# The first head pair's choice of clusters in two halves of 384 queries and 384 keys

## The chip, the cores and the metric

The kernel runs on one core of a Trainium2 chip. The time is the device time of one execution in microseconds (us). The time before is the median of three runs, 702.19 us (699.18, 702.19 and 703.92).

Engines: TensorE (PE in the profile, its weight loads PEld), VectorE (DVE), ScalarE (ACT), GpSimd (POOL) and SyncE (SP, which here only issues transfers).

## What is computed

Attention in which a query sees only the keys of its own cluster, and behind it a mixture of experts in which each row goes to one expert:

```python
# q, k, v: (4, 8, 768, 64); centroids: (8, 16, 64); x: (3072, 512); 8 experts of 512 x 1024 x 512
q_assign = np.argmax(np.einsum('bhsd,hcd->bhsc', q_n, c_n), axis=-1)
k_assign = np.argmax(np.einsum('bhsd,hcd->bhsc', k_n, c_n), axis=-1)
mask = q_assign[:, :, :, None] == k_assign[:, :, None, :]
scores = scale * np.matmul(q, k.transpose(0, 1, 3, 2))
scores = np.where(mask, scores, -1000000000.0)
...
return np.matmul(attn, v).astype(np.float32)
...
logits = xn @ en.T / tau
expert_idx = np.argmax(logits, axis=1)
...
h = np.maximum(x[mask] @ w1[e], 0.0)
out[mask] = gate_w[mask, None] * (h @ w2[e])
```

Here q_n, k_n, c_n, xn and en are rows divided by their length, attn is the softmax of the scores and gate_w the softmax of the logits at the chosen expert.

## The kernel before

The 32 pairs of batch and head are worked through as 16 pairs of heads (n = 0 to 15), two heads side by side in the 128 rows of TensorE. Of each pair, 768 queries are taken in two halves of 384 (`hq`), and for each half the 768 keys in six blocks of 128 (`j`). One such block is a *unit*; there are 12 to a pair, and the main loop takes two units a step (`it` = 0 to 5). For a unit, `scores` fills one tile of PSUM (s_ps, L519) from two parts: part 1 is the product of k and q (f32), part 0 the product of the *table* H (bf16, `hot` in the profile), which adds a large negative number where the clusters of query and key differ. `expo` (L530, ScalarE) makes the exponential, `attend` (L541) multiplies by v on TensorE, and VectorE sums the exponentials for the softmax (L550 and L560).

The table of a pair is made in *pieces*, which stand in the program ahead of the pair's own units:

- *turn*: q and k are turned so that the head's 64 numbers lie along the partitions. From pair 1 on VectorE does it in blocks of 32 (L402). For pair 0 TensorE turns them with the identity (L383) and VectorE and ScalarE copy the results out of PSUM (L389, L393).
- *products* (L412): the product with the unit centroids, cnB, four matmuls of 384 columns (two halves of q, two of k), then a transpose by VectorE into asn (L421).
- *choose* (L430 to L433, VectorE): the largest of 16 per row, as a number pm.
- *codes* (L438, L442): from pm the entries of cd, for queries and keys; the constant entries of cd are written once, in `constants`.
- the table: cd turned. From pair 1 on a transposing transfer does it (L456); for pair 0 TensorE does (L467, `turn_numbers`), and VectorE and ScalarE copy parts of it into `hot` (L474 to L479).

In pair 0, before, the two halves of k's turned columns are not natural halves: `in_halves` places alternate groups of 32 keys, and v is loaded in the matching order (eight transfers, L196).

The start is written out by hand in `begin()`, and the whole attention stage runs under a manual schedule: every engine runs its instructions in the order of the program text. TensorE first runs ten dummy products (`keep_up`, L233), later six more while the choice is made. A transfer is issued by an engine's own queue (here SP's or ScalarE's); its end is told by one of eight semaphores that are used in turn, so that an issue can wait for the end of the transfer that had its semaphore before. `misc()` gives two PSUM banks in turn; psS has two more for the scores (used for q's turn at the start), and unit 2's scores at the start take a tile of the values products' pool.

The changed places by line: `load` L190, `keep_up` L229, `constants` L252, `unit_centroids` L301, `unit_experts` L313, `turned_experts` L318, `begin` L328, `turn` L373, `choose` L423, `codes` L436, `turn_numbers` L458, `scores` L499, `between` L1369 and the main loop from L1430.

Of the kernel before, what the change touches and what calls it, by code (L numbers as in the profile page):

```python
# [39 lines left out]
def kernel(  # L40
# [144 lines left out]
    def load(n, names):  # L185
        b, hp = pairs[n]
        t = ld.setdefault(n, {})
        for nm in names:
            x = t[nm] = ldp.tile([P, NJ, 2, D], F32, tag=nm + "32", name=nm + "32")
            for h in range(2):  # L190
                rows = {"q": q, "k": k, "v": v}[nm][b, 2 * hp + h]
                if nm == "v":
# [7 lines left out]
                if n == 0:  # L200

                    for i in range(1 + (nm == "k")):
                        js = slice(NJ // 2 * i, NJ // 2 * i + NJ // 2) if nm == "k" else slice(0, NJ)
                        queue = nc.scalar if nm == "k" and i == 0 else nc.sync
                        queue.dma_start(
                            out=x[:, js, h], in_=rows.rearrange("(j p) d -> p j d", p=P)[:, js]
                        )
                    continue


# [42 lines left out]
    def constants():  # L253
        nc.vector.memset(onesb, 1.0)
        keep_up(10, idle_ps[:, 0])
# [45 lines left out]
    def unit_centroids():  # L301
        unit_rows(cn_r)
        nc.vector.tensor_scalar(cn2, bc(c_sb, [P, 2, D], 1), cn_r, None, ALU.mult)
        bk = misc()
# [8 lines left out]
    def unit_experts():  # L313
        unit_rows(en_r)
        nc.vector.reciprocal(tau, tau)
        nc.vector.tensor_scalar(emb, emb, en_r, tau, ALU.mult, ALU.mult)

    def turned_experts():  # L318
# [5 lines left out]
        nc.vector.tensor_copy(  # L324
# [3 lines left out]
    def begin():  # L328

        nc.scalar.dma_start(out=c_sb, in_=centroids.rearrange("h c d -> (h c) d"))  # L330
        load(0, "q")
        load(0, "k")
        nc.sync.dma_start(out=emb, in_=moe_expert_emb)
        nc.sync.dma_start(out=tau, in_=moe_tau.to_broadcast([E, 1]))
        load(0, "v")
        load(1, "qk")
        constants()

        nc.scalar.activation(en_r, epsc[0:E], ACTF.Sqrt)
        norm_rows(cn_r, c_sb, P)  # L340
        unit_centroids()
        piece(0, "turn0")
        piece(0, "turn1")
        norm_rows(en_r, emb, E)

        nc.scalar.activation(cn_r, epsc, ACTF.Exp)
        piece(0, "products")
        for m in range(2):
            scores(m, (1,))
        un[2]["s_ps"] = psO.tile([P, 2, 512], F32, tag="o_ps", name="s_ps2")  # L350
        scores(2, (1,))
        piece(0, "choose")
        piece(0, "codes")
        keep_up(6, misc())
        unit_experts()
        rest = piece(0, "turn_numbers")
        next(rest)
        for m in range(3):
            scores(m, (0,))
        next(rest, None)  # L360
        turned_experts()
        for m in (0, 2, 1):
            expo(m)
        token_numbers()

    def prep_pieces(n):
# [8 lines left out]
        def turn(nm, half):  # L375
# [12 lines left out]
            if nm == "q":  # L388
                (nc.vector.tensor_copy if half else nc.scalar.copy)(  # L389
                    t["qT"][:, HS * half : HS * half + HS], bk[:, 0:HS]  # L390
                )
            else:
                (nc.scalar.copy if half else nc.vector.tensor_copy)(  # L393
                    in_halves(t["kT"])[:, half], bk[:, 0:HS].rearrange("p (s t) -> p s t", t=SQ)
                )
# [27 lines left out]
        def choose():  # L423
# [3 lines left out]
            amax = smp.tile(shp[0:2], F32, tag="amax", name="amax")  # L427
            sel = smp.tile(shp, BF16, tag="sel", name="sel", bufs=1)
            pm = smp.tile(shp[0:2], BF16, tag="pm", name="pm")
# [6 lines left out]
        def codes():  # L436
            pm = t["pm"]
            nc.scalar.activation(cd[..., 1], pm, ACTF.Copy, scale=wcd)  # L438
# [1249 lines left out]
```

## Time and profile before

| | us |
|---|---|
| median of three runs | 702.19 |
| the profiled execution | 699.54 |
| its span | 697.7 |
| TensorE busy in the span | 684.7 (98%) |
| VectorE, ScalarE, GpSimd busy | 381.4, 261.5, 252.7 |
| granted TensorE clock, mean of the span | 0.999 |

The profile is of one execution. A page gives the busy time of each engine, the chain of work that ended last, followed back from the end, and groups of instructions by line; a row of a group has the count, the busy time in us, the mean of one in ns, and the idle time ahead of it with what ended it. The trace behind it can be asked for any stretch. In the first 16 us, by the timeline (start, length):

| | us |
|---|---|
| dummies of L233 | 1.07, 3.71 |
| centroids turned, L305 | 5.17, 0.30 |
| q turned, L383 | 5.33, 0.85 |
| k turned, L383, two halves | 6.12 and 6.89, 0.52 each |
| centroid products, L412 | 7.38 to 8.82 |
| asn, L421 | 8.85, 0.58 |
| amax, is_equal, product, pm, L430 to L433 | 9.47, 10.05, 10.64, 11.04 |
| codes on VectorE, L442, two | 11.70, 0.53 |
| cd turned, L467 | 12.38, 0.83 |
| copies to the table, L474 to L479 | 13.15 to 14.19 |
| scores, part 0, units 0 to 2 | 13.95, 0.68 |
| exponentials of units 0, 2, 1, 3 | 14.36, 2.92 |
| attend of units 0 and 1 | 16.03, 1.80 |

### The profile page before, as it was taken

To read this page: it belongs to the slowest core of one execution; us is meant where nothing else is said; L and a number is where in the kernel's file an instruction comes from. 1 tells how busy PE (TensorE), PEld (TensorE's weight loads), DVE (VectorE), ACT (ScalarE), POOL (GpSimd) and SP (SyncE) were. 2 spreads that over 40 slices of the span, in tenths; PEclk is the share of its full clock that TensorE was granted. 3 is DMA by queue.
4 is the path that set the end of the run, shared out by engine and by line. 5 is a ranking of instruction groups with operands and counts; after the bars stand their busy time and mean duration, and the time that the engine had idled before them with its cause. 6 is when DMAs were issued, how large, how long until landed. Compare 5 with 4: busy or idle time off the path is not lost.

```text
span 697.7 us, 16185 instructions
## 1 busy us (share of the span) xinstructions
PE 684.7 (98%) x6517; PEld 459.1 (66%) x6517; DVE 381.4 (55%) x667; ACT 261.5 (37%) x443; POOL 252.7 (36%) x439
## 2 busy tenths in 40 slices
PE   8999999999999999999999999998999999999996
PEld 4444444444444444456776678887979797979694
DVE  6788998998899999988563121240210303030310
ACT  5656655577666765576142120101010111111111
POOL 2122222321132222361216256736364554635402
PEclk9999999999999999999999999999999999999999
DMA  8755566875578587699699957457777686879450
GB/s 136 121 90 108 103 98 82 163 142 104 107 134 165 122 154 149 173 277 260 171 357 353 348 172 284 158 192 244 260 249 268 218 296 236 294 265 317 143 226 32
DMA packets 244156, 135.55 MB, mean 194 GB/s; under 512 B 207840, under 2 KB 207842, under 8 KB 244076
## 3 DMA queue, kind: packets, MB, share of 16 engines
q1 hardware_dynamic: 237116, 121.10, 63.9%
q0 software_dynamic: 6016, 13.12, 5.2%
q8 instruction: 54, 0.88, 0.6%
q10 hardware_dynamic: 944, 0.23, 0.2%
q14 instruction: 26, 0.21, 0.1%
HBM read 115.92 MB, written 13.12 MB: 185 GB/s over the span
## 4 chain that ended last, share of the span: by engine, by line
PE 89%; issue 4%; DMA 3%; POOL 1%; DVE 1%; another core or an unknown queue 1%; POOLq 0%; ACT 0%; DVEq 0%
PE s_ps L519 22%; PE o_ps L541 18%; PE h_ps L1303 10%; PE y_ps L1319 10%; PE h_ps L1217 9%; PE y_ps L1254 5%; PE misc L1254 5%; PE x_ps L1217 3%; DMA out_dram<-ys,spidx 3%; PE misc L591 2%; PE misc L412 2%; PE misc L670 1%; POOL out_dram L1090 0%; POOL xin L1079 0%
## 5 line engine op out<-in xcount | busy, mean ns | idle before, releaser
L530 ACT ACTIVATE prob<-s_ps 128x768 f32<-128x768 f32 x192 | 154.1, 814 | 100.8 <-PE s_ps L519 99.9
L519 PE MATMUL s_ps<-qT,kT 64*64 64x384 f32 x1536 | 155.6, 482 | 0.0
L541 PE MATMUL o_ps<-prob,v 64*64 64x385 f32 x1536 | 141.2, 483 | 0.0
L560 DVE TENSOR_TENSOR acc<-acc,prob 128x768 f32<-128x768 f32 x128 | 121.6, 950 | 8.5
L541 PEld LDWEIGHTS o_ps<-prob,v 64*64 64x64 f32 x1536 | 58.4, 133 | 65.0 <-issue 57.8
L1263 DVE STREAM_TRANSPOSE ys<-y_ps 128x256 f32<-128x256 f32 (+4 forms) x16 | 6.5, 414 | 156.8 <-PE y_ps L1254 141.1
L1303 PE MATMUL h_ps<-xTm,w1s 128*128 128x128 f32 x768 | 89.0, 276 | 1.2 <-issue 1.2
L1303 PEld LDWEIGHTS h_ps<-xTm,w1s 128*128 128x128 f32 x768 | 87.6, 192 | 3.0 <-issue 2.6
L1319 PE MATMUL y_ps<-w2s,hT 128*128 128x512 f32 x192 | 84.5, 593 | 0.0
L1090 POOL DMA_INDIRECT out_dram<-ys,spidx x56 | 56.3, 1005 | 74.7 <-DVE ys L1277 58.7
L519 PEld LDWEIGHTS s_ps<-qT,kT 64*64 64x64 f32 x1536 | 55.2, 133 | 36.9 <-issue 32.3
L1217 PE MATMUL h_ps<-xTs,w1s 128*128 128x272 f32 (+7 forms) x384 | 72.9, 346 | 1.1 <-ACTq L1577 1.1
L1217 PEld LDWEIGHTS h_ps<-xTs,w1s 128*128 128x128 f32 x384 | 66.6, 190 | 8.0 <-issue 2.4
L575 POOL COPY behind<-acc 1x1 f32<-1x1 f32 x30 | 6.7, 223 | 177.9 <-DVE acc L560 169.1
L1310 ACT ACTIVATE hT<-h_ps 128x512 f32<-128x512 f32 x24 | 14.3, 596 | 146.1 <-PE h_ps L1303 136.3
L519 PE MATMUL s_ps<-hot 64*64 64x384 bf16 x768 | 64.2, 325 | 1.0 <-DVE hot L478 0.7
L1079 POOL DMA_INDIRECT xs<-x_rows,gpidx x56 | 56.6, 1010 | 17.1 <-issue 16.8
L1319 PEld LDWEIGHTS y_ps<-w2s,hT 128*128 128x128 f32 x192 | 35.6, 190 | 40.2 <-issue 40.2
L519 PEld LDWEIGHTS <-hot 64*64 64x64 bf16 x768 | 23.8, 106 | 43.8 <-issue 41.8
L1254 PE MATMUL y_ps<-hTs,w2o 128*128 128x272 f32 (+7 forms) x256 | 48.2, 346 | 0.2 <-issue 0.2
L1254 PE MATMUL misc<-hTs,w2o 128*128 128x272 f32 (+7 forms) x256 | 48.0, 346 | 0.0
L1254 PEld LDWEIGHTS y_ps<-hTs,w2o 128*128 128x128 f32 x256 | 44.4, 190 | 2.9 <-issue 0.4
(273 smaller groups left out, 694.9 us busy)
## 6 DMA issues: line engine op xcount, KB each, us to landing
w1s<-in_moe_w_dram SPq DMA_DIRECT2D x18, 2048.0 KB
w2s<-in_moe_w_dram SPq DMA_DIRECT2D x18, 2048.0 KB
v<-in_v_dram SPq DMA_DIRECT2D x128, 48.0 KB
k<-in_k_dram SPq DMA_DIRECT2D x62, 96.0 KB
q<-in_q_dram SPq DMA_DIRECT2D x60, 96.0 KB
x_rows<-xb SPq DMA_DIRECT2D x60, 96.0 KB
xr<-x_rows SPq DMA_DIRECT2D x9, 512.0 KB
w1s<-in_moe_w_dram SPq DMA_DIRECT2D x4, 1024.0 KB
```

Source lines behind the costliest of these rows:

```text
L412: nc.tensor.matmul(bk[2 * C * i : 2 * C * i + 2 * C, 0:HS], lhsT=cnB[:, hp], rhs=r, start=True, stop=True,)
L519: nc.tensor.matmul(s_ps[D * half : D * half + D, h, 0:HS], lhsT=l[rows, half], rhs=r[rows], start=part == (1 if len(parts) < 2 else 0), st ...
L530: nc.scalar.activation(d["prob"][:, :, 0:HS], d["s_ps"][:, :, 0:HS], ACTF.Exp, scale=scale)
L541: nc.tensor.matmul(g["o_ps"][D * h : D * h + D, half, 0:HE], lhsT=ld[n]["v"][keys, j, h], rhs=d["prob"][keys, h, 0:HE], start=(j == 0), st ...
L560: nc.vector.tensor_tensor(g["acc"], g["acc"], d["prob"][:, :, 0:HS], ALU.add)
L1079: nc.gpsimd.indirect_dma_start(out=to, out_offset=None, in_=of, in_offset=bass.IndirectOffsetOnAxis(ap=at, axis=0), bounds_check=n - 1, oo ...
L1090: inst = nc.gpsimd.indirect_dma_start(out=to, out_offset=bass.IndirectOffsetOnAxis(ap=at, axis=0), in_=of, in_offset=None, bounds_check=n - 1,
L1217: nc.tensor.matmul(bk, lhsT=w1s[it.slot][:, c, P * f : P * f + P], rhs=d["xT"][:, c, 0:C], start=(c == 0), stop=(c == KD - 1),)
L1254: nc.tensor.matmul(bks[g][:, 0:C], lhsT=d["w2"][:, f, P * g : P * g + P], rhs=d["hT"][:, f, 0:C], start=(f == 0), stop=(f == KF - 1),)
L1303: nc.tensor.matmul(bk[:, m : m + P], lhsT=w1s[it.slot][:, c, f0 + m : f0 + m + P], rhs=d["xT"][:, P * c : P * c + P], start=(c == 0), stop ...
L1310: nc.scalar.activation(d["hT"][:, f0 : f0 + 512], bk, ACTF.Relu)
L1319: nc.tensor.matmul(bk, lhsT=d["hT"][:, P * c : P * c + P], rhs=w2s[it.slot][:, c], start=(c == 0), stop=(c == KF - 1),)
```

## The change

Pair 0 is loaded and prepared in two halves: natural queries 0 to 383 and keys 0 to 383, then the rest.

- `load`: for pair 0, SP's queue takes half 0 of q and k of both heads, then half 1 (eight transfers of 98 KB; before, q in two of 196 KB and k in four of 98 KB, two of them by ScalarE's queue). v of pair 0 comes in natural order in two transfers. The experts' embeddings and tau move to ScalarE's queue.
- `turn` copies into natural columns and leaves the engine of the copy to the caller. The centroids are turned behind the first halves.
- `half_products`, `choose(half)`, `codes(half)` and `table(half)` do the work of one half: 192 columns instead of 384, 12 groups instead of 24, six turns of cd in two banks instead of twelve. The middle code goes from ScalarE to GpSimd. Each bank of the table is copied out whole (384 columns), one by VectorE, one by ScalarE.
- `scores` of pair 0 reads the queries of its half from that half of the table.
- `begin` runs half 0 through to the table, has the scores of units 0 and 2 and their exponentials in between, then half 1 and unit 1. The experts' scaling, before one operation of VectorE over 8 x 512, becomes two of VectorE on 8 x 1 and one of ScalarE over 8 x 512. Eight dummies are left at the start, the six later ones are gone.
- In the main loop the scores of unit 3 stand between attend(0) and attend(1), pair 1's products behind the scores of units 4 and 5, and the token numbers at pair 0's step 4.

```diff
-    def load(n, names):
+    def load(n, names, halves=(0, 1)):
         b, hp = pairs[n]
         t = ld.setdefault(n, {})
         for nm in names:
-            x = t[nm] = ldp.tile([P, NJ, 2, D], F32, tag=nm + "32", name=nm + "32")
+            if nm not in t:
+                t[nm] = ldp.tile([P, NJ, 2, D], F32, tag=nm + "32", name=nm + "32")
+            x = t[nm]
             for h in range(2):
                 rows = {"q": q, "k": k, "v": v}[nm][b, 2 * hp + h]
+                if n == 0:
+                    x_h, rows = x[:, :, h], rows.rearrange("(j p) d -> p j d", p=P)
+                    if nm == "v":
+                        nc.sync.dma_start(out=x_h, in_=rows)
+                        continue
...
-                if n == 0:
-
-                    for i in range(1 + (nm == "k")):
-                        js = slice(NJ // 2 * i, NJ // 2 * i + NJ // 2) if nm == "k" else slice(0, NJ)
-                        queue = nc.scalar if nm == "k" and i == 0 else nc.sync
-                        queue.dma_start(
-                            out=x[:, js, h], in_=rows.rearrange("(j p) d -> p j d", p=P)[:, js]
-                        )
-                    continue
-
...
-        keep_up(10, idle_ps[:, 0])
+        keep_up(8, idle_ps[:, 0])
...
+    def turned_centroids():
...
     def unit_experts():
-        unit_rows(en_r)
-        nc.vector.reciprocal(tau, tau)
-        nc.vector.tensor_scalar(emb, emb, en_r, tau, ALU.mult, ALU.mult)
+        nc.vector.tensor_scalar(en_r, en_r, 1e-6, tau, ALU.add, ALU.mult)
+        nc.vector.reciprocal(en_r, en_r)
...
     def begin():
 
         nc.scalar.dma_start(out=c_sb, in_=centroids.rearrange("h c d -> (h c) d"))
-        load(0, "q")
-        load(0, "k")
-        nc.sync.dma_start(out=emb, in_=moe_expert_emb)
-        nc.sync.dma_start(out=tau, in_=moe_tau.to_broadcast([E, 1]))
+        nc.scalar.dma_start(out=emb, in_=moe_expert_emb)
+        nc.scalar.dma_start(out=tau, in_=moe_tau.to_broadcast([E, 1]))
+        for half in range(2):
+            load(0, "qk", (half,))
         load(0, "v")
         load(1, "qk")
         constants()
 
-        nc.scalar.activation(en_r, epsc[0:E], ACTF.Sqrt)
+        nc.scalar.activation(cn_r, epsc, ACTF.Sqrt)
         norm_rows(cn_r, c_sb, P)
+        norm_rows(en_r, emb, E)
         unit_centroids()
-        piece(0, "turn0")
-        piece(0, "turn1")
-        norm_rows(en_r, emb, E)
-
-        nc.scalar.activation(cn_r, epsc, ACTF.Exp)
-        piece(0, "products")
-        for m in range(2):
-            scores(m, (1,))
+        piece(0, "turn", "q", 0)(nc.vector.tensor_copy)
+        piece(0, "turn", "k", 0)(nc.scalar.copy)
+        turned_centroids()
+        unit_experts()
+        junk = smp.tile([P, 1], F32, name="junk1", bufs=1)
+        nc.scalar.activation(junk, epsc, ACTF.Exp)
+        piece(0, "half_products", 0)
+        piece(0, "turn", "q", 1)(nc.scalar.copy)
+        evict = piece(0, "turn", "k", 1)
+        piece(0, "choose", 0)
+        piece(0, "codes", 0)
+        evict(nc.scalar.copy)
+        scores(0, (1,))
+        evicts = piece(0, "table", 0)
+        evicts[0](nc.vector.tensor_copy)
+        evicts[1](nc.scalar.copy)
+        nc.scalar.activation(emb, emb, ACTF.Copy, scale=en_r)
+        piece(0, "half_products", 1)
         un[2]["s_ps"] = psO.tile([P, 2, 512], F32, tag="o_ps", name="s_ps2")
         scores(2, (1,))
-        piece(0, "choose")
-        piece(0, "codes")
-        keep_up(6, misc())
-        unit_experts()
-        rest = piece(0, "turn_numbers")
-        next(rest)
-        for m in range(3):
-            scores(m, (0,))
-        next(rest, None)
-        turned_experts()
-        for m in (0, 2, 1):
-            expo(m)
-        token_numbers()
+        scores(0, (0,))
+        expo(0)
+        piece(0, "choose", 1)
+        scores(2, (0,))
+        expo(2)
+        scores(1, (1,))
+        piece(0, "codes", 1)
+        evict = turned_experts()
+        evict()
+        evicts = piece(0, "table", 1)
+        evicts[0](nc.vector.tensor_copy)
+        evicts[1](nc.scalar.copy)
+        scores(1, (0,))
+        expo(1)
...
-            if nm == "q":
-                (nc.vector.tensor_copy if half else nc.scalar.copy)(
-                    t["qT"][:, HS * half : HS * half + HS], bk[:, 0:HS]
-                )
-            else:
-                (nc.scalar.copy if half else nc.vector.tensor_copy)(
-                    in_halves(t["kT"])[:, half], bk[:, 0:HS].rearrange("p (s t) -> p s t", t=SQ)
-                )
+            to = t[nm + "T"][:, HS * half : HS * half + HS]
+            return lambda copy: copy(to, bk[:, 0:HS])
...
+        def half_products(half):
+
+            W = HS // 2
+            bk = misc()
+            for i in range(4):
+                r = in_halves(t["qT" if i < 2 else "kT"])[:, i % 2]
+                nc.tensor.matmul(
+                    bk[2 * C * i : 2 * C * i + 2 * C, 0:W],
+                    lhsT=cnB[:, hp],
+                    rhs=r[:, W // SQ * half : W // SQ * half + W // SQ],
+                    start=True,
+                    stop=True,
+                )
+            if half == 0:
+                t["asn"] = smp.tile([P, HS], F32, tag="asn", name="asn", bufs=1)
+            nc.vector.transpose(t["asn"][:, W * half : W * half + W], bk[:, 0:W])
...
+            if half is not None:
+                g = slice(S // SQ // 2 * half, S // SQ // 2 * (half + 1))
+                asn, amax, sel, pm = asn[:, g], amax[:, g], sel[:, g], pm[:, g]
+                shp = [P, S // SQ // 2, C]
...
+        def codes(half=None):
             pm = t["pm"]
-            nc.scalar.activation(cd[..., 1], pm, ACTF.Copy, scale=wcd)
-            for i, p0 in enumerate((0, D)):
-                g = slice(p0, p0 + D)
-                if n == 0:
+            if half is not None:
+                U = S // (4 * SQ)
+                to = cd[:, U * half : U * half + U]
+                nc.gpsimd.tensor_scalar(to[..., 1], pm, wcd, None, ALU.mult)
+                for i, p0 in enumerate((0, D)):
+                    g = slice(p0, p0 + D)
                     nc.vector.scalar_tensor_tensor(
-                        out=cd[g, :, :, 2 * i],
+                        out=to[g, :, :, 2 * i],
                         in0=pm[g],
                         scalar=(BIG, 1.0)[i],
                         in1=pm[g],
                         op0=ALU.mult,
                         op1=ALU.mult,
                     )
-                    continue
+                return
...
+        def table(half):
 
             U = S // (4 * SQ)
+            if half == 0:
+                t["H"] = trp.tile([P, S // (2 * SQ), P], BF16, tag="hot", name="hot")
+            copies = []
+            for s0 in (U * half, U * half + U // 2):
+                bk = misc().bitcast(BF16)[:, 0 : P * U // 2]
+                for u in range(U // 2):
                     nc.tensor.transpose(
                         bk[:, P * u : P * u + P],
+                        cd[:, s0 + u].rearrange("p h c -> p (h c)"),
                         identb,
                     )
+                H = t["H"][:, s0 : s0 + U // 2].rearrange("r s x -> r (s x)")
+                copies.append(lambda copy, H=H, bk=bk: copy(H, bk))
+            return copies
...
+                U = S // (4 * SQ)
                 r = t["H"][:, :, SQ * hq : SQ * hq + SQ]
+                if n == 0:
+                    r = t["H"][:, U * hq : U * hq + U, 0:D]
...
+            elif it == 4:
+                token_numbers()
...
-            for m in range(i + 2 if i else 3, min(i + 4, len(units))):
+            for m in range(i + 2 if i else 4, min(i + 4, len(units))):
...
+            if (n, it) == (0, 1):
+                piece(1, "products")
...
                 attend(m)
+                if m == 0:
+                    scores(3, (1,))
+                    scores(3, (0,))
+                    expo(3)
...
-            if it == 0:
+            if it == 0 and n > 0:
                 piece(n + 1, "products")
```

## The prediction

> **What bounds the kernel now.** I read the page's busy shares first, then the busy time by stretches, then the chain of waits, then the start instruction by instruction. The page, and the stretches (length, busy us of PE, PEld, DVE, ACT, POOL, granted clock, DMA share, GB/s):
>
> ```profile
> PE 684.7 (98%) x6517; PEld 459.1 (66%) x6517; DVE 381.4 (55%) x667; ACT 261.5 (37%) x443; POOL 252.7 (36%) x439
> ```
>
> ```profile
> 0.00:4.80 4.80, 3.71 (x10) 1.24 (x10) 1.64 (x13) 1.93 (x5) 3.77 (x17) 1.00 0.70 141
> ...
> 8.80:16.00 7.20, 6.14 (x71) 3.02 (x71) 5.84 (x21) 3.99 (x7) 0.00 (x0) 1.00 1.02 146
> 16.00:24.00 8.00, 8.00 (x104) 3.85 (x104) 7.55 (x11) 4.31 (x8) 0.00 (x0) 1.00 0.82 122
> 24.00:100.00 76.00, 76.00 (x1060) 36.83 (x1056) 65.75 (x86) 46.98 (x68) 18.58 (x76) 1.00 0.57 100
> ```
>
> From 16 us on TensorE has no gap; from 16 to 690 us its idle time is 4.7 us (365.3 busy of 370 behind 320 us, the rest full). Before 16 us it is busy too, but partly with the dummy products of L233. So the change can only move the moment at which the gapless stretch begins, and what it gains there should reach the end. The chain of waits shows that moment (start, length, link):
>
> ```profile
> 7.41 1.41 PE misc L412 x8
> 8.82 0.02 issue
> 8.85 0.60 DVE asn L421
> 9.44 0.02 issue
> 9.47 0.56 DVE amax L430
> ...
> 12.69 0.53 DVE emb L316
> 13.22 0.17 DVE hot L474
> ...
> 13.95 0.39 PE s_ps L519 x4
> ...
> 18.66 1.74 PE s_ps L519 x24
> 20.40 1.29 PE o_ps L541 x16
> ```
>
> The reader should see: products at 7.4, then 3.4 us of VectorE alone (8.85 to 12.23) for choice and codes, then table and copies until 13.95. I take **20.40 us, the start of the values products of units 2 and 3, as the mark**: before and after, exactly units 0 to 5's scores, attend(0), attend(1) and pair 1's centroid products stand ahead of it, and the order behind it is the same.
>
> **What the loads set.** The trace's landing records give q at 3.84 and 5.19, the four k loads at 4.29, 5.98, 6.33 and 6.76. TensorE turns q at 5.33 and the two k halves at 6.12 and 6.89, so each turn starts 0.13 us behind its load. Landed bytes against time (98 KB for half a load): 229 KB at 3.84, 327 at 4.29, 523 at 5.19, 817 at 6.76. The change sends 98 KB q0, q0, k0, k0, q1, q1, k1, k1, all on SP's queue, with emb and tau on ScalarE's. With 33 KB of centroids and 16 of emb beside them, the first four are 441 KB: by that curve about 4.8 us; the last, 835 KB, about 6.9. SP issues one such load in 0.49 to 0.54 us (four from 0.76 on end at 2.9), so the issue is no tighter. Three of the last four wait for a reused semaphore, of c_sb (2.94), a q0 load and emb (about 3.8 by the curve), and their turns to issue come at 3.5, 4.0 and 4.6: nothing. Queued behind them on SP are v and pair 1's loads. v becomes two issues instead of eight (3.9 us), pair 1's eight loads begin about 6.1 instead of 8.78, and the first v reader comes at 13.7: hidden.
>
> **Half the data is not half the time.** VectorE's reduction over 384 columns and over 192:
>
> ```profile
> L430 DVE TENSOR_REDUCE amax<-asn 128x24 f32<-128x384 f32 x16 | 8.8, 553 | 0.6
> L939 DVE TENSOR_REDUCE destb<-wb 128x24 f32<-128x192 f32 x1 | 0.4, 353 | 0.0
> ```
>
> A half costs 0.353, not 0.277: 0.20 saved. The whole chain takes 3.38 us; four f32-sized operations (asn, amax, is_equal, pm) save 0.20 each, the bf16 product of 0.36 about 0.13, the two code writes (0.26 each at 24 columns) almost nothing: 3.38 - 0.95 = **2.4 us for each half, 4.8 for both**. POOL now writes the middle code (128x12): nearest rows are its 32x12 copy, 0.26, and 128x8 bf16 product, 0.40. It starts with VectorE's two code writes (0.52), which hide it; without that cover it costs 0 to 0.4 a half. If SBUF traffic between the two slows both, the bound is the same 0.4; I take 0.
>
> **The new start, step by step.**
> - Eight dummies end about 4.35 (ten end at 4.78). ScalarE issues three small loads where it issued c_sb and two of k, so c_sb's norm is not later: cn2 at 5.0 or earlier.
> - q0 turned from 4.35, copied by VectorE until 5.5 (0.56); k0 turned from 4.9 (load plus 0.13) to 5.4, copied by ScalarE until 5.95 (0.48; emb's norm, 1.0 us, ends before); cn2's turn next, cnB's two copies (0.46) until 6.2.
> - Half products at 6.25. Pair 1's whole products take 17.75 to 18.71 up to asn, their matmuls 0.65 of it (a chain row, 37.04 to 37.69); half is 0.96 - 0.33 = 0.63, asn starts 6.9 (before: 8.85). Codes of half 0 are written at 6.9 + 2.4 = **9.3** (before: 12.23).
> - Under that chain TensorE turns q1 and k1 (0.14 x 6) and does scores(0)'s q-k part (0.64 a unit: 1.93 of the 2.17 for three at 8.74). ScalarE's Exp table (1.28) runs from 5.95; its copies of q1 and k1 are done at 8.2, in cover.
> - Three turns of cd for each bank: first bank at 9.65, VectorE's copy of 384 bf16 columns 0.34 (0.236 for 192 and 0.434 for 576 give 0.335): 10.0. The second bank's goes to ScalarE, 0.48, until 10.25. The expert scaling (0.53 on VectorE, in the chain before, at 12.69) is now on ScalarE in the shade, ahead of expo(0).
> - Half products of half 1 reuse that bank and stand in TensorE's queue **behind** the turns of cd: 10.05. asn at 10.7, codes of half 1 at **13.1**. So the two VectorE chains run one after the other with 1.4 us between them, and TensorE covers the second with only scores(2), scores(0)'s table part, scores(1)'s q-k part and emb's turn, about 2.2 us from 10.4, and waits some 0.5 us.
> - Turns of cd 13.15, scores(1)'s table part 13.5, attend(0) 13.7 to 14.35, scores(3) (0.81) to 15.15. ScalarE: half 1's copy 13.65 to 14.13, expo(1) (0.81) until 14.95. attend(1) 15.15 to 15.8, scores(4) and (5) (1.61) to 17.4, pair 1's products (0.65 to 0.84) to 18.1. The mark is at **18.1 instead of 20.40: 2.3 us gained.**
>
> Edits at nothing: token numbers (0.71 of VectorE) leave 15.12 to 15.93, where they hold pair 1's turns, for pair 0's fifth step; there VectorE has 3.07 busy of 6 us (24 to 30), and without that slack they cost 0.7. VectorE gains only about 1 us on pair 1's choice, because products(1) come one step later; the third prob buffer is wanted at about 22.6 and its sum is done at 21.3, so no wait, but 0 to 1 if VectorE runs late. Six dummies between scores and codes go: they filled a wait and cost nothing, except for the clock.
>
> **The clock.** Dummies' weight loads:
>
> ```profile
> 1.90 0.15 PEld L233 LDWEIGHTS <-onesb 128*128 128x128 bf16 x1 [0.28 <-issue]
> ...
> 3.61 0.15 PEld L233 LDWEIGHTS <-onesb 128*128 128x128 bf16 x1 [0.27 <-issue]
> 3.97 0.31 PEld L233 LDWEIGHTS <-onesb 128*128 128x128 bf16 x2 [0.21 <-issue]
> ```
>
> They go at 0.43 us until 3.6 and then faster (the six at 10.84 take 1.47, 0.245 each): full speed comes 2.9 us after the first, and eight dummies still reach that (7 x 0.43 + 1.07 = 4.08). Behind it the longest TensorE gap in my plan is about 0.9 us, at 8.4. So I price the dummies at nothing. [...]
>
> **Sum.** The profiled execution took 699.54 us (span 697.7 plus 1.8 around it), 2.65 under the median of the three runs, 702.19. Minus 2.3 it would be 697.2; on the median, **699.9 us**.
>
> **Rivals.**
> 1. The gain is mostly given back at the second half (under 1 us left): every half operation near its full price adds 1.0 a chain, both chains lie in series: 2.3 - 2.0 = 0.3 us, time 701.9. For it: the 1.4 us hole and the ScalarE queue (expo(0), expo(2), copy, expo(1)) ahead of attend(1). Against: the 0.353 row. It includes k1 landing late: all eight loads are on one queue, and turns of k1 stand ahead of the turns of cd; it decides from a landing at about 8.6, against 6.9.
> 2. Larger: loads land at the issue rate (k0 at 4.4) and half chains take 2.0: 0.4 + 0.8 more, 3.5 us, time 698.7.
> 3. Slower: the clock stays at half after eight dummies. It needs 4.6 us of critical TensorE work at half clock to eat 2.3 us. Between 4.4 and 18.1 my plan holds 10.3 us of such work; if it is cold up to attend(0), about 5 us double: 5 - 2.3 = 2.7 lost, time 704.9. For it: two fewer dummies and none later. Against: the rise at 3.9 us.
> That the change does not do what it says can be left out: the order of instructions of the changed kernel shows both halves as described.
>
> **How the numbers follow.** Forecast (1 to 3.4 us gained) 0.72; rival 1 0.16; rival 2 0.06; rival 3 0.06. The three runs lie from 3.0 under to 1.7 over their median, as much as the whole effect. Range: 702.2 - 3.5 - 2.4 = 696.3 to 702.2 - 0.3 + 1.4 = 703.3. One per cent, 7 us, is about what a measurement can tell from no change, and half of the whole start; only scatter or a cold clock gets there: faster 0.03, same 0.95, slower 0.02.
>
> **What would show it.** Right: asn of half 0 near 6.9, codes at 9.3 and 13.1, the mark at 18.1, a gapless TensorE behind it and the same sequence to the end. Wrong: dummy-like 0.43 us spacing or doubled matmuls after 4.4 us; k1's turn behind 8.6; half reductions over 0.45; TensorE idle behind the mark, or the saving found at 100 us and gone at 690.

## Result and profile after

| | us |
|---|---|
| changed kernel, median of 22 runs (698.01 to 705.03) | 700.77 |
| kernel before, 22 runs beside them (697.6 to 706.19) | 699.89 |
| ratio, 95% interval | 1.0015 [0.9997, 1.0034] |
| profiled execution of the changed kernel, its span | 705.03, 702.6 |
| the same two kernels on another chip (chip 6 below): changed, before | 693.63, 694.56 |
| ratio there | 0.9987 [0.9978, 0.9996] |

No change that counts by one per cent. The profiled execution after is 5.5 us longer than the one before (699.54), although its start is shorter. The chain of waits of the changed kernel, from the half products on (start, length, link):

```profile
6.59 0.57 PE misc L436 x8
...
7.25 0.39 DVE asn L445
...
9.44 0.22 DVE cd L476
9.66 0.14 issue
9.80 0.34 PE misc L503 x3
...
10.16 0.37 DVE hot L509
...
10.57 0.58 PE misc L436 x8
...
11.18 0.39 DVE asn L445
...
13.28 0.20 DVE cd L476
13.49 0.14 issue
13.62 0.49 PE misc L503 x6
...
14.41 0.65 PE o_ps L577 x8
...
18.12 0.78 PE misc L419 x8
18.90 1.45 PE o_ps L577 x16
```

The last row is the mark, 20.40 before: 1.50 us gained by these rows, 1.40 by the first instruction of each, which I use below (kernel before, then changed):

```profile
20.23 1.46 PE L541 MATMUL o_ps<-prob,v 64*64 64x385 f32 x16
```

```profile
18.83 1.52 PE L577 MATMUL o_ps<-prob,v 64*64 64x385 f32 x16
```

The two VectorE chains stand one behind the other as planned, 7.25 to 9.66 and 11.18 to 13.48, and between them lie a turn, a copy and the second half's products.

Busy time by stretches (length, PE, PEld, DVE, ACT, POOL, granted clock, DMA share, GB/s), changed kernel:

```profile
8.80:16.00 7.20, 5.52 (x76) 2.94 (x80) 5.37 (x15) 3.89 (x7) 0.72 (x2) 1.00 1.50 144
16.00:24.00 8.00, 8.00 (x112) 3.68 (x108) 5.74 (x10) 5.08 (x9) 0.00 (x0) 1.00 0.63 101
24.00:100.00 76.00, 76.00 (x1060) 37.15 (x1056) 68.25 (x91) 46.92 (x69) 18.56 (x76) 1.00 0.59 100
100.00:320.00 220.00, 219.69 (x3070) 106.93 (x3069) 201.94 (x297) 142.72 (x223) 61.97 (x158) 1.00 0.73 154
320.00:690.00 370.00, 362.81 (x2167) 304.69 (x2160) 95.88 (x238) 57.08 (x126) 166.04 (x180) 0.99 0.71 245
```

Behind the mark TensorE is full again until 100 us; 0.31 us are missing from 100 to 320, and in the experts' stretch it does 362.81 us of work where before did 365.34, at a granted clock of 0.99. The longest of TensorE's waits in that stretch, changed kernel (waited for: total, times, longest):

```profile
PE x_ps L1253 <- ACT hTs L1260: 4.7, 2, 2.5
```

and the kernel before:

```profile
PE x_ps L1217 <- ACT hTs L1224: 2.1, 1, 2.1
```

ScalarE stands 3.9 us ahead of each of them. The profile names no releaser, but the only semaphore that the waiting copy needs is TensorE's, and the products that the first of these copies reads end at 479.10 in the trace, 6.6 us ahead of its start (the ends of products are modelled). The wait near 486 is in both kernels (2.1 to 2.2 us). In the changed kernel alone the granted clock then falls to half, from 486.09 to 489.50 and, behind the second wait, from 530.46 to 533.88:

```profile
486.00:488.00 2.00, 1.88 (x5) 1.63 (x6) 0.00 (x0) 0.86 (x4) 0.00 (x0) 0.52 0.00 0
...
530.00:532.00 2.00, 1.79 (x5) 1.65 (x6) 0.00 (x0) 0.90 (x4) 0.00 (x0) 0.62 0.04 8
```

Matching instructions of the two profiled executions stand apart by -1.40 us at the mark, -1.28 from 41 to 182 us, -1.08 behind 193, -0.72 behind 259, -1.03 at 484, +0.65 behind 489, +4.88 behind 534 and +4.86 at the end. So three questions: why 1.4 and not 2.3 at the mark; where half of it goes by 257 us; whether the waits at 486 and 530 belong to the change.

### The profile page after: what moved, and what is told of

Read it like the earlier page. It is cut to its first block, busy times and chain, and to the rows that moved or that the text cites. A ratio compares the mean times of both kernels' runs of the same rounds, so it can differ in the third digit from the quotient of the medians.

```text
span 702.6 us, 16188 instructions
## 1 busy us (share of the span) xinstructions
PE 685.9 (98%) x6517; PEld 461.1 (66%) x6517; DVE 381.7 (54%) x669; ACT 262.5 (37%) x445; POOL 253.0 (36%) x441
## 4 chain that ended last, share of the span: by engine, by line
PE 85%; issue 5%; DMA 4%; DVE 2%; another core or an unknown queue 1%; ACT 1%; POOL 1%; POOLq 0%; SPq 0%; DVEq 0%; ACTq 0%
PE s_ps L555 21%; PE o_ps L577 17%; PE h_ps L1339 10%; PE y_ps L1355 10%; PE h_ps L1253 8%; PE y_ps L1290 5%; PE misc L1290 5%; PE x_ps L1253 4%; DMA out_dram<-ys,spidx 3%; PE misc L627 2%; PE misc L419 1%; PE misc L706 1%; DMA q<-in_q_dram 1%; DMA k<-in_k_dram 0%
## 5 line engine op out<-in xcount | busy, mean ns | idle before, releaser
(273 smaller groups left out, 699.9 us busy)
```

## Experiments

These ran on three other chips, called 6, 1 and 4 here; the kernel before takes 694.56, 694.63 and 694.72 us on them, so their times are compared with each other. "Cut" means that the head pairs behind the one named, the end of the routing and the experts are left out:

```diff
             n, it = divmod(i // 2, NJ)
+            if n == 4:
+                break
...
+        nc.sync.dma_start(out=out[0:P, 0:HS], in_=gr[2 * 4 - 1]["acc"][:, 0])
```

### Start and end apart: both kernels cut, and both whole (chip 6)

> The kernel before, left after the fourth head pair: attention of pairs 4 to 15 and the whole expert stage are left out, and the last pair's softmax sums are written in place of the result. It gives the start and four pairs by themselves, about 95 us, with the same start as before (values products of units 2 and 3 at 20.2 us). Theory A (the start's gain is real and lasts, the expert stage hides it): it is 1.4 us slower than its partner with the change. Theory B (the gain is given back inside attention, by VectorE's later choice for pair 1 or by transfers): the two differ by under 0.5 us.

> The changed kernel, left after the fourth head pair in the same way (pairs 4 to 15 and the expert stage left out). Theory A: 1.4 us (1.1 to 1.7) under the kernel before cut in the same place, and the profile has no TensorE idle time between 19 us and the end. Theory B: within 0.5 us of it.

> The kernel before against itself: ratio 1.000, within 0.004. Its profile tells how often the expert stage has a wait of about 4 us for a late TensorE semaphore and whether the granted clock drops behind it. Theory A (such waits come at random in either kernel): 0 to 2 of them, and a slow profile has more of them. Theory C (the change causes them): none or one without a clock drop, as in the first profile of before.

> The changed kernel once more. Theory A: ratio 0.996 to 1.003; the mark (values products of units 2 and 3) at 18.8 again; the number of 4 us waits in the expert stage is 0 to 2 and not the same as in its first profile. Theory C: two waits with clock drops at the same places (near 486 and 530 us) again, and a ratio of 1.002 to 1.006.

The cuts take 96.88 us (96.59 to 96.91) and 95.46 (95.33 to 95.52): **1.42 us** gained and kept to the end of the cut. Their marks are 20.49 and 18.79; this 1.70 holds a late rise of the clock in the profiled execution of the kernel before (6.80 us, against 3.89 to 5.71 in its other traces). The whole kernels take 694.56 (21 runs) and 693.63: **0.93 us** gained. Neither trace has a wait of TensorE for hTs or a fall of the clock in the experts' stretch (granted 1.00 from 320 to 470, 470 to 540 and 540 to 685 us in both). The list of TensorE's waits behind 320 us, changed kernel on chip 6, is one line:

```profile
PE h_ps L1253 <- ACTq L1621: 1.1, 1, 1.1
```

So the change does not by itself bring on the two waits, and the reading that it costs 5 us at the end falls. Between these two traces the distance is -1.28 at the mark, -1.22 from 41 to 182 us, -1.02 behind 193, -0.65 behind 259 and -0.67 at the end: the shrinking ahead of 260 us is there again.

### Is k's first half what the half products wait for? (chip 1)

```diff
-                        nc.sync.dma_start(out=x_h[:, js], in_=rows[:, js])
+                        queue = nc.scalar if nm == "k" and half == 0 else nc.sync
+                        queue.dma_start(out=x_h[:, js], in_=rows[:, js])
...
+        for half in range(2):
+            load(0, "qk", (half,))
         nc.scalar.dma_start(out=emb, in_=moe_expert_emb)
         nc.scalar.dma_start(out=tau, in_=moe_tau.to_broadcast([E, 1]))
-        for half in range(2):
-            load(0, "qk", (half,))
```

> The changed kernel cut behind the fourth head pair (the rest of the heads, routing and experts are left out), with the two k loads of half 0 on ScalarE's queue ahead of the experts' loads, so that they are sent beside q's and not behind them. Beside the same cut with SP sending all (95.46 us, mark 18.79). Theory A (the landing of k's half 0, 5.18 us where I forecast 4.8, sets the half products): k lands about 4.4, the mark comes 0.3 to 0.4 earlier, about 18.4, and the time is about 95.1 us. Rival B (VectorE's queue sets them: copy of q's turn from 5.33, then the two copies of the turned centroids until 6.40, products at 6.54, whatever k does): products stay within 0.1 us of 6.54 if q lands as before, and later by as much as q does; the mark stays within 0.15 us of 18.8, the time at 95.3 to 95.6 us.

96.31 us, 0.85 **more**; neither theory said so. k's half landed at 5.03 instead of 5.13: two queues hardly brought these bytes sooner. But ScalarE has its own work behind its issues. Its timeline here (start, length):

```profile
1.19 0.99 ACTq L202 DMA_DIRECT2D k<-in_k_dram  x2
2.21 0.64 ACTq L335 DMA_DIRECT2D emb<-in_moe_expert_emb_dram  x1
3.00 0.30 ACTq L336 DMA_DIRECT2D tau<-in_moe_tau_dram  x1
3.33 1.28 ACT L341 ACT_TABLE_LOAD   x1 [3.33 <-DMA q<-in_q_dram]
```

and in the cut of the change:

```profile
1.81 0.31 ACTq L333 DMA_DIRECT2D tau<-in_moe_tau_dram  x1
2.15 1.28 ACT L340 ACT_TABLE_LOAD   x1 [2.15 <-issue]
```

Two loads put ahead of a table load move it by 1.18 us, and with it the centroids' norm, their turn (5.63 to 6.21) and the products (6.54 to 7.18). k's turn itself hardly moved (5.27 to 5.16). The theory that k's landing alone sets the start isn't supported; the run could not test it cleanly, since k landed only 0.1 us earlier. What it shows is a second path that is not much shorter, the centroids': delayed by 1.18 us it made the products 0.64 later, so it had about 0.5 us to spare.

### How much is the side edit? (chip 1)

The cut of the kernel before, with the change's scaling of the expert embeddings alone:

```diff
     def unit_experts():
-        unit_rows(en_r)
-        nc.vector.reciprocal(tau, tau)
-        nc.vector.tensor_scalar(emb, emb, en_r, tau, ALU.mult, ALU.mult)
+        nc.vector.tensor_scalar(en_r, en_r, 1e-6, tau, ALU.add, ALU.mult)
+        nc.vector.reciprocal(en_r, en_r)
...
         unit_experts()
+        nc.scalar.activation(emb, emb, ACTF.Copy, scale=en_r)
         rest = piece(0, "turn_numbers")
```

> The kernel before, cut behind the fourth head pair in the same way, with one side edit of the change alone: VectorE's scaling of the expert embeddings (0.53 us in front of its first table copy) becomes one small multiply-add, one reciprocal and a ScalarE copy with a scale. No halves. The cut before takes 96.88 us, mark 20.49. Theory A (the side edit is worth what VectorE had in front of the table copy): first table copy 0.4 to 0.6 us earlier, mark 0.3 to 0.5 earlier, time 96.4 to 96.6 us, so about a third of the change's 1.42 us is not from halving. Rival B (the table's turns or ScalarE set that moment): time within 0.15 us of 96.88.

96.56 us (96.53 to 96.71), 0.32 less; mark 20.16, table copy from 13.41 to 12.98. But the turns of cd ahead of that copy were also 0.19 us earlier in this trace, which the edit can't do. So the edit is worth 0.1 to 0.3 of the 1.42 us: as measured at the low end of what Theory A said, and below it without the 0.19.

### How much is the halving of the chain? (chip 1, with the dummies chip 4)

The cut of the change, with the loads, turns, products and table still in halves, but the choice made over all rows at once:

```diff
-        piece(0, "choose", 0)
-        piece(0, "codes", 0)
...
         piece(0, "half_products", 1)
...
         scores(2, (1,))
...
+        scores(1, (1,))
+        piece(0, "choose")
+        pm = ld[0]["pm"]
+        for half in range(2):
+            ld[0]["pm"] = pm[:, 6 * half : 6 * half + 6]
+            piece(0, "codes", half)
+        keep_up(6, misc())
...
```

The first run was without the last line, the second with it.

> The changed kernel cut behind the fourth head pair, with loads, turns, centroid products and first transposes in halves as in the change, but choice over all 768 rows at once, then the codes, then the table; scores of units 0, 2 and 1 from q and k stand ahead of them. Beside the cut of the change (95.46 us, mark 18.79). Theory A (the gain is the first half's chain running while the second half is loaded and turned): choice starts about 9.6 instead of 7.6 and takes the whole 2.1 to 2.3 us, the table's first turns come about 12.3, the mark at 19.7 to 20.3, the time at 96.3 to 97.0 us: most of the 1.42 us goes. Rival B (the earlier loads and the cheaper codes brought it, not the halves of the chain): mark within 0.4 us of 18.8, time under 95.9 us.

> The same as the run with the whole chain (changed kernel cut behind the fourth head pair, choice over all rows at once), with the six dummy products of the kernel before put back on TensorE behind the scores, ahead of the table's turns. Without them TensorE stood still from 10.0 to 12.3 and its clock fell to half from 15.45 to 18.87; the cut took 98.47 us. Theory A (without halves the chain costs what it did in the kernel before, and the clock's fall came on top): no fall at 15 us, table turns at 12.3 as before, mark 19.6 to 20.2, time 96.3 to 96.9 us. Rival B (the halves of the loads alone keep the gain): time under 95.9 us.

Without the dummies 98.47 us, above even the cut of the kernel before. TensorE's timeline (start, length, idle before):

```profile
8.93 1.52 PE L553 MATMUL s_ps<-qT,kT 64*64 64x384 f32 x16
12.32 0.49 PE L501 MATMUL misc<-identb,cd 128*128 128x128 bf16 x6 [1.87 <-DVE cd L474]
...
15.74 1.56 PE L575 MATMUL o_ps<-prob,v 64*64 64x385 f32 x8 [0.70 <-ACT prob L564]
```

It waits 1.87 us for the codes, and the clock fell to half from 15.45 to 18.87 in this very stretch (attend(0) takes 1.56 instead of 0.8):

```profile
15.40:18.80 3.40, 3.06 (x24) 1.36 (x28) 2.58 (x3) 0.99 (x2) 0.00 (x0) 0.51 1.12 107
```

All five executions without the dummies have a mean granted clock of 0.958 to 0.982, the five of the cut of the change 1.000. With the dummies the profiled execution kept its clock: 96.50 us, mark 20.07, as Theory A had it. Another run took 96.67; the other two took 98.12 and 99.05, with mean granted clocks of 0.982 and 0.971, so the median, 97.40, is not the price of the chain alone. The marks of the profiled one and of the cut of the change:

```profile
20.07 1.52 PE L576 MATMUL o_ps<-prob,v 64*64 64x385 f32 x16
```

```profile
18.79 1.52 PE L577 MATMUL o_ps<-prob,v 64*64 64x385 f32 x16
```

20.07 - 18.79 = **1.28 us of the change's gain come from the halved chain, at the least**: the execution with the whole chain had the earlier start (clock up at 3.83 against 5.22, half products at 6.07 against 6.54), and from the half products on the difference is 14.00 - 12.25 = 1.75 us. Of the 1.70 us between the marks of the two cuts that leaves at most 0.4 for everything else, the side edit included. And the halves keep TensorE out of the long wait behind which the clock fell.

### Where it is given back: both kernels cut behind pair 13 (chip 4)

> The kernel before, cut behind the thirteenth head pair (the other pairs, the end of the routing and the experts are left out), as the measure for the next run: about 267 to 275 us. In the whole kernel's traces its matching instructions at 257 us lie 0.65 us later than the changed kernel's, those at 190 us 1.0 us later, those at 20 us 1.3 us later.

> The changed kernel, cut behind the thirteenth head pair in the same way. Theory A (VectorE and ScalarE set the pace in the second eight head pairs, so that an earlier start is partly given back there): 0.4 to 0.9 us less than the kernel before cut there. Rival B (the shift read from one pair of traces is scatter; what is gained at the start is passed on whole): 1.2 to 1.6 us less.

273.60 us (273.45 to 274.60) and 272.62 (271.87 to 272.81): 0.98 us, between the two theories and next to the whole kernels' 0.93. So by these times about 0.45 us of the 1.42 are given back ahead of 272 us and nothing measurable behind it. By the traces it is 0.56: this pair stands apart by -1.24 at the mark, -1.23 up to 182 us, -1.04 behind 193 and -0.67 behind 259, and the other two pairs lose 0.20 and 0.36 or 0.37 us at the same two places. The cause of the loss near 190 us is open. Near 257 the changed kernel's only TensorE wait between 30 and 266 us, where the kernel before has none, is:

```profile
PE s_ps L555 <- ACT prob L566: 0.3, 1, 0.3
```

ScalarE's timeline ahead of it:

```profile
254.88 0.40 ACT L485 ACTIVATE cd<-pm,wcd 128x24 bf16<-128x24 bf16 x1 [0.59 <-DMA v<-in_v_dram]
255.10 0.61 ACT L488 ACTIVATE cd<-pm 64x24 bf16<-64x24 bf16 x2
255.74 0.81 ACT L566 ACTIVATE prob<-s_ps 128x768 f32<-128x768 f32 x1
```

The code writes stand in ScalarE's queue ahead of an exponential that TensorE's next bank waits for, and they start 0.04 us behind VectorE's choice (pm ends at 254.84), so I read the choice as their releaser rather than the DMA named. VectorE had lost its lead before: at 237.75 an addition to acc waits 0.46 us, which it doesn't in the kernel before. VectorE there is the engine with the least slack beside TensorE (changed kernel, then before, 240 to 266 us; the third busy time is VectorE's):

```profile
240.00:266.00 26.00, 25.71 (x368) 12.55 (x360) 24.86 (x43) 15.65 (x23) 4.23 (x13) 1.00 0.80 175
```

```profile
240.00:266.00 26.00, 26.00 (x376) 12.87 (x372) 24.82 (x44) 15.78 (x26) 4.68 (x14) 1.00 0.85 179
```

What releases the addition at 237.75 is not settled: the profile names ScalarE's copy of o_sb, but in the kernel before the same addition starts ahead of that copy's end. So the place of the loss is shown, and its way to TensorE read from the traces; that VectorE's load causes it is not shown, since no run took work off VectorE.

### A regrouped start (the cut on chip 1, the whole kernel on chip 4)

In the cut of the change TensorE stands idle between 8.8 and 14 us for 1.4 us (3.76 busy of 5.20; not the 2.1 of the expectation below), nearly all of it ahead of the turns of cd and of the second half's products. The turns wait for the codes, the products for a bank that VectorE's copy must free (changed cut, TensorE):

```profile
9.75 0.49 PE L503 MATMUL misc<-identb,cd 128*128 128x128 bf16 x6 [0.76 <-DVE cd L476]
10.53 0.36 PE L436 MATMUL misc<-qT,cnB 128*32 128x192 f32 x2 [0.28 <-DVE hot L509]
...
13.58 0.49 PE L503 MATMUL misc<-identb,cd 128*128 128x128 bf16 x6 [0.40 <-DVE cd L476]
```

The second half's q and k had been ready since 8.7. So its products were put ahead of the first half's turns, its choice directly behind the first half's codes, and other scores into the waits:

```diff
         scores(0, (1,))
-        evicts = piece(0, "table", 0)
-        evicts[0](nc.vector.tensor_copy)
-        evicts[1](nc.scalar.copy)
         nc.scalar.activation(emb, emb, ACTF.Copy, scale=en_r)
         piece(0, "half_products", 1)
         un[2]["s_ps"] = psO.tile([P, 2, 512], F32, tag="o_ps", name="s_ps2")
         scores(2, (1,))
+        for evict in piece(0, "table", 0):
+            evict(nc.scalar.copy)
+        piece(0, "choose", 1)
+        scores(1, (1,))
+        evict = turned_experts()
         scores(0, (0,))
         expo(0)
-        piece(0, "choose", 1)
         scores(2, (0,))
         expo(2)
-        scores(1, (1,))
         piece(0, "codes", 1)
-        evict = turned_experts()
         evict()
-        evicts = piece(0, "table", 1)
-        evicts[0](nc.vector.tensor_copy)
-        evicts[1](nc.scalar.copy)
+        for evict in piece(0, "table", 1):
+            evict(nc.vector.tensor_copy)
+        scores(3, (1,))
         scores(1, (0,))
...
```

(`table(0)` turns its six blocks into one bank; the main loop's q-k part of scores(3) goes.)

> The changed kernel cut behind the fourth head pair, with the second half's work moved forward: its centroid products stand ahead of the first half's table turns on TensorE, its choice follows the first half's codes directly on VectorE, the first table half is turned into one bank and copied by ScalarE alone, the scores of units 2, 1 and 3 from q and k fill TensorE's waits for the tables. Beside the cut of the change (95.46 us, mark 18.79, in which TensorE stands still some 2.1 us between 8.8 and 14.0). Theory A (the second half's chain waits for VectorE's table copy and for a bank, not for data: products of half 1 ready from 8.75, run at 10.53): codes of half 1 at about 11.9 instead of 13.2, mark 17.3 to 17.9, time 94.0 to 94.6 us. Rival B (a new wait takes its place, the expected one being ScalarE's single copy of the first table half, some 0.85 us, ahead of the exponentials): mark 18.4 to 19.0, time 95.1 to 95.7 us.

> The whole kernel with the regrouped start of the cut (second half's centroid products ahead of the first half's table turns, its choice directly behind the first half's codes, first table half copied by ScalarE alone). The cut gained 0.83 us over the cut of the change and 2.25 us over that of the kernel before. Theory A (what a start gains is passed on but for 0.5 to 0.8 us that the later pairs give back): 1.3 to 1.9 us less than the kernel before, ratio 0.9973 to 0.9981, mark 17.8 to 18.2. Rival B (VectorE's and ScalarE's queues in the later pairs hold a floor that the change has already reached): no more than 1.0 us less than the kernel before, as the change itself (0.93 us).

The cut takes 94.63 us (94.10 to 94.89), mark 17.97: 0.83 us better, between the theories and nearer to A. The codes of half 1 start at 11.41 and end at 11.84, as A had them; the rest of A's gain is lost at TensorE, which waits for a bank until expo(0) has read it, and puts unit 3's scores ahead of unit 1's table part. The whole kernel takes **692.69 us (692.28 to 692.95) against 694.72: 2.03 us less, ratio 0.9969 [0.9958, 0.9981]**, the best of the three and slightly over A's 1.3 to 1.9. Its TensorE at the start, whole kernel:

```profile
8.92 0.36 PE L435 MATMUL misc<-qT,cnB 128*32 128x192 f32 x2
...
9.38 0.88 PE L555 MATMUL s_ps<-qT,kT 64*64 64x384 f32 x8
10.19 0.51 PE L503 MATMUL misc<-identb,cd 128*128 128x128 bf16 x6
10.63 0.88 PE L555 MATMUL s_ps<-qT,kT 64*64 64x384 f32 x8
...
12.40 0.49 PE L503 MATMUL misc<-identb,cd 128*128 128x128 bf16 x6
13.05 0.88 PE L555 MATMUL s_ps<-qT,kT 64*64 64x384 f32 x8 [0.15 <-ACT prob L566]
```

The bracketed waits of 0.76, 0.28 and 0.40 are gone. Its lead over the kernel before (chip 6's trace) is 2.18 us at the mark, 2.11 from 41 to 250 us and 1.74 behind 259: near 257 us the later pairs take 0.37 us from this start too, with the same wait of 0.46 us ahead of the same addition, near 190 us they take nothing, and no floor holds the rest. The loss is thus not a share of the lead.

## Why the prediction came out as it did

**The number.** 699.9 us and no change by one per cent, measured 700.77. The nearness of the numbers is luck: I subtracted 2.3 us from a median of three runs, 702.19; the kernel before took 699.89 in 22 runs beside the changed one, 2.3 us less, and at the end no gain showed on that chip, so that two errors nearly cancel. The forecast was of a gain of 1 to 3.4 us; at the mark it is there (1.4, 1.3, 1.2 in three pairs of whole or 13-pair traces), at the end 0.93 on one chip and not to be seen on the other.

**The mechanism and the half chain: right.** The chain of half 0, from asn at 7.25 to the codes' end at 9.66, takes 2.41 us; I had 2.4 from the 0.353 row. GpSimd's middle code (9.20 to 9.57) ends before VectorE's two (9.20 to 9.66) and is hidden. The second half's products do stand behind the turns of cd. q1's and k1's turns, the table load and the token numbers are in cover, and TensorE has no gap from the mark to 100 us. That the halved chain makes most of the gain is shown by the run with the whole chain.

**"2.3 us gained" at the mark: a size, 0.8 to 0.9 too much.** By the chain the mark is at 18.90 against my 18.1. By differences of my steps from the rows: +0.36 up to the codes of half 0 (half products 6.59, not 6.25); +0.17 at the first table half, where I left out the 0.14 between codes and turns; -0.14 over the second half's products and chain (2.91 us, I had 3.05); +0.24 at the second table half, where 0.14 of issue and six turns of 0.49 had got 0.4 together; +0.09 at the table part of scores(1) and +0.09 behind attend(1).

**"Half products at 6.25" needs an early clock and an early k.** I priced the dummies at nothing because the rise came 2.9 us after the first. In the runs it came between 3.83 and 6.97 us, 2.8 to 5.9 behind the first dummy at 1.05. I read 4.8 for the landing of k's half from the curve of landed bytes; it was 4.67 to 5.18. The program is the same up to the half products in these eight executions (us):

| execution | rise of the clock | k's half landed | half products |
|---|---|---|---|
| whole chain, with the dummies | 3.83 | 4.67 | 6.07 |
| the change, first chip | 4.81 | 5.18 | 6.59 |
| whole chain, without them | 5.21 | 4.69 | 6.39 |
| the change, cut behind pair 4 | 5.22 | 5.13 | 6.54 |
| regrouped, cut | 5.32 | 4.78 | 6.45 |
| the change, cut behind pair 13 | 6.02 | 4.99 | 6.82 |
| the change, chip 6 | 6.14 | 4.98 | 6.84 |
| regrouped, whole | 6.97 | 4.74 | 6.78 |

Where k landed late (5.13 and 5.18) or the clock rose first (3.83), the products start 1.40 to 1.41 us behind k's landing; in the other five the clock rose behind 5.2 and the slow turns hold them. The earliest, with the dummies' whole chain (rise 3.83; start, length):

```profile
4.14 0.49 PE L395 MATMUL q_ps<-ident,q 128*128 128x128 f32 x3
4.81 0.52 PE L395 MATMUL misc<-ident,k 128*128 128x128 f32 x3 [0.17 <-DMA k<-in_k_dram]
...
6.07 0.36 PE L435 MATMUL misc<-qT,cnB 128*32 128x192 f32 x2 [0.64 <-DVE cnB L310]
```

and the regrouped kernel (rise 6.97):

```profile
4.44 0.85 PE L395 MATMUL q_ps<-ident,q 128*128 128x128 f32 x3
5.08 0.85 PE L395 MATMUL misc<-ident,k 128*128 128x128 f32 x3
5.72 0.42 PE L307 MATMUL misc<-ident,cn 128*128 128x128 f32 x1
6.78 0.43 PE L435 MATMUL misc<-qT,cnB 128*32 128x192 f32 x2 [0.64 <-DVE cnB L310]
```

In the regrouped kernel the turns take 0.85 us instead of 0.5, and VectorE's copies behind them pass this on. In all these runs but the earliest the eight dummies were over (at 4.64 or 4.65 us in four of them, by the modelled ends) before the clock rose (4.81 or later); in the earliest the rise came 2.78 us behind the first dummy (3.83 and 1.05). What brings the rise is not shown. None came later than 6.97 us, and the gain at the mark was there in every trace of the change. Two fewer dummies did not move the rise either way that these runs could tell: in the kernel before, with ten, it came at 3.89, 5.35, 5.71 and 6.80.

**"What it gains there should reach the end": half to two thirds.** 0.93 of 1.42 us by the times on the other chips, 0.65 of 1.22 by the traces of chip 6. I took a full TensorE for a queue that passes everything on. From 100 to 320 us VectorE is busy 202 of 220 us as well, and 0.56 us of the lead are lost there in each of three pairs of traces, at two places; that VectorE is the cause is my reading of the second of them. I had named "found at 100 us and gone at 690" as a sign of error and priced nothing for it.

**Rivals.** Rival 1's size (under 1 us left) is what stands at the end, but its mechanism, the second half's operations at full price or k1 landing late, is not: half 1's chain takes 2.3 us, and k1 landed at about 6.8. Rival 2's terms, k0 at 4.4 and half chains of 2.0, didn't come either (4.67 at the earliest, 2.3 and 2.4). Rival 3, the cold clock until attend(0), didn't occur: the latest rise came at 6.97.

**Open.** On the first chip the ratio, 1.0015, excludes the other chip's 0.9987. That chip's executions scatter over 7 to 9 us; those of the changed kernel with the longest times (704.2 to 705.0) have mean granted clocks of 0.994 or 0.995, the shortest 1.000. The one trace of the changed kernel there loses 5.9 us in the experts' stretch (from -1.03 to +4.88), by one wait more than before and two falls of the clock. Whether a start 1.4 us earlier makes these waits and falls likelier on that chip was not tried; on the other chips no trace of either whole kernel has one.

## What to carry to other kernels

A full first engine does not pass an earlier start on whole: here 0.56 us of 1.2 went in the later stretches, and 0.37 of 2.1 from a better start. Look for the busiest second engine in each later stretch, and price a loss there; it need not be a share of the gain. When a step is split in halves, draw each engine's queue for both halves together; here the second half waited for a bank and a queue place, not for its data, and moving its work forward doubled the gain (0.93 to 2.03 us). And price work near the rise of the clock from both sides, with the rise early and late (3.83 and 6.97 us here), and not by one execution.

## What the runs showed of the hardware

- **The changes of the clock lay whole multiples of one length apart.** Between two changes in a trace lay 10.24 us (5.21 to 15.45, the whole chain without dummies), 40.96 and 481.28 (489.50 to 530.46 and 4.81 to 486.09, the change on the first chip), 88.75 (3.83 to 92.58, the whole chain with dummies) and 692.91 (3.89 to 696.80, the kernel before on the first chip): by division 3, 12, 141, 26 and 203 times 3.413. The three falls inside a kernel last 3.41 to 3.42 us each (486.09 to 489.50, 530.46 to 533.88, 15.45 to 18.87), and the first of them cost 1.68 us (the distance to the kernel before, which has the same wait without a fall, granted clock 1.00 from 484 to 490, goes from -1.03 to +0.65). The rise lay between 3.83 and 6.97 us, 3.14 apart. TensorE was not idle ahead of the falls: in the 3.41 us ahead of those at 486.09 and 530.46 it was busy 1.28 and 0.89 us, and ahead of the one at 15.45 2.15 us, of which 1.4 were turns (0.49, 0.51 and 0.41). What sets off a fall is not shown: the kernel before was busy 1.28 of the 3.40 us from 485.00 on as well, and its clock stayed at 1.00 up to 490.
- **A wait behind products that had ended by the trace.** Near 482 to 486 us ScalarE waits 3.9 us for TensorE's semaphore, in both profiled executions on the first chip (copies at 485.70 and, before, 486.70), though by the trace's modelled ends the products are done (at 479.10 and 480.13). The memory traffic runs at about 400 GB/s up to the start of the wait (373 from 480 to 482 us in the changed kernel) and at 98 and 33 in the two slices of 2 us behind it. A further trace of the changed kernel (span 691.4 us) has a like stretch (377, 110 and 33 GB/s in the slices of 2 us from 478 to 484) and no such wait, TensorE 2.00 busy of 2.00 in each, so the traffic alone does not make it. The cause is not shown.
- **A DMA issue on ScalarE isn't free at the start.** Two loads of 98 KB took 0.99 us of its queue, pushed a table load by 1.18 us, and the cut took 0.85 us longer.
